# The silu's add of one on POOL in two of four channel blocks, and DMA transposes and DMA adds kept strictly apart

## Chip, cores and metric

The kernel runs on one core of one Trainium2 chip. The metric is the device time of one execution in microseconds (us).

## What is computed

Two sequences of 16000 steps with 512 channels go through a depthwise convolution of three taps, a silu, four stages of residual quantisation with eight code words each, and a second depthwise convolution on the chosen words. Inputs and outputs are bf16.

```python
B, T, D, K = 2, 16000, 512, 3
Nq, C = 4, 8

def reference(x, dw_enc, codebooks, dw_dec):
    ...
    for i in range(K):
        z = z + xp[:, i:i+T, :] * dw_enc[i][None, None, :]
    z = _silu(z)
    res = z
    q = jnp.zeros_like(z)
    for s in range(Nq):
        cb = codebooks[s]
        d2 = jnp.einsum("btd,btd->bt", res, res)[..., None] - 2.0 * jnp.einsum("btd,cd->btc", res, cb) + jnp.einsum("cd,cd->c", cb, cb)[None, None, :]
        idx = d2.argmin(-1)
        sel = cb[idx]
        q = q + sel
        res = res - sel
    qp = jnp.pad(q, ((0,0),(pad,pad),(0,0)))
    for i in range(K):
        y = y + qp[:, i:i+T, :] * dw_dec[i][None, None, :]
    return y
```

## The kernel before

**Tiles.** The 32000 steps are 250 groups of 128, cut into 16 chunks: one of 12 groups, fourteen of 16, one of 14 (which is treated as 16 in the first part). Channels lie on the partitions in four blocks (`i` from 0 to 3), so a tile of one block of one chunk is 128 x 2048.

**The first part, `front`.** For each chunk, DMA transposes on the SP queue bring the input from HBM with channels on partitions into XT (`run`, L486, up to four groups each, two XT buffers; 74 in all and one edge). Chunk 0 is transposed by PE instead. Then, for each of the four blocks (`block`): DVE multiplies by the three taps (`product`, L553, out to Z and to two tiles T); the products are added up (`total`), by DVE (L561) or by an accumulating DMA on the POOL queue (L559). From chunk 1 on (`EARLY = 1`) the first of a block's two sums is a DMA in all four blocks and the second in block 3 (`DMA_ADDS`): five a chunk, 75 in all. The silu follows as exp on ACT (L565, E from Z), an add of one on DVE (`one`, L569, E in place), a logarithm on ACT (L573, LN from E), exp of its negative on ACT (L576), and the product with Z on DVE (`silu`, L581, into RES).

**The second part, `stage`, four times a chunk.** PE scores the residual against the code words (L643, into PS), DVE takes norm and products out (L651, L654), combines them (L673, L679, L684), finds the least (L689) and writes a one-hot row (L697), which PE turns (L707) and DVE copies (L714). PE then multiplies it with the words; the residual RES is brought up to date either by DVE (L747, from SEL in PSUM) or by PE and an ACT copy (L752, L758). At the end `outputs` decodes on PE (L785), copies with ACT to YSB (L791, three buffers) and stores from the SP queue (L795).

**The order of the work.** It is planned ahead, when the program is built. Every step is a task with an engine, the time that it holds the engine, the time until its result is there, and a due time (`Plan.add`). `pass_over` plays the tasks through forwards or backwards by rank; `run` repeats that for each entry of `ROUNDS` (a seed, two spreads for the random shift of the ranks, and a number of passes), each from the order of the one before. `emit` writes the instructions out in the order of planned starts, and each engine runs its own in that order. All DMAs are one engine of the plan, "DMA". Transposes are of kind 1 there (`RUNS`), accumulating DMAs of kind 2 (`ADDS`), stores of none; between a DMA of one kind and one of the other the plan leaves `APART` us, and weighs such a pause with `CLUMP` when it picks. A picked DMA is listed at the moment when it is picked, the pause included in the time that it holds the plan's engine. POOL is an engine of the plan of its own, though the accumulating DMAs are issued from its queue.

`keep_apart` makes the program hold to that on the chip: a transpose waits for an accumulating DMA, and the other way round, where `others` are those of the other kind issued so far.

```python
if len(others) >= LAG:
    tc.add_manual_dep(t.ins, others[-LAG].name, ...)
mine.append(t.ins)
```

With `LAG = 2` it waits for the last but one of the other kind.

Of the kernel before, what the change touches and what calls it, by code (L numbers as in the profile page):

```python
# [13 lines left out]
ALU = mybir.AluOpType  # L14
# [21 lines left out]

EARLY = 1

RUN = 4

AHEAD = 40
# [2 lines left out]
PERIOD, LEAD, STAGE, LATE, SPREAD = 56, 0.4, 0.9, 0.3, 0.3  # L44
FAR = -3.3e38

ROUNDS = [(940, 0.3, 0.0, 7), (4101, 0.3, 2.0, 9), (5991, 0.3, 0.0, 7), (15520, 0.3, 0.0, 10)]


CELLS, COLUMNS, ROWS = range(3)  # L50
WHOLE = (CELLS, CELLS, 0, 0.0)
SWITCH, CLING, SLOW = 0.1, 10.0, 1.08
RUNS, ADDS = (1, 1, 0, 0.0), (2, 2, 0, 0.0)
APART, CLUMP = 0.5, 2.0

LAG = 2


class Plan:
# [18 lines left out]
    def pass_over(self, rank, backward=False):  # L78

        tasks = self.tasks  # L80
        needs = [t[3] for t in tasks]
        after = [[] for _ in tasks]
        for n, ds in enumerate(needs):
            for d in ds:
                after[d].append(n)
        if backward:
            needs, after = after, needs
        takes, gives = (7, 6) if backward else (6, 7)
        left = [len(d) for d in needs]
        engines = list(dict.fromkeys(t[0] for t in tasks))  # L90
        ready = {e: [] for e in engines}
        until = {e: 0.0 for e in engines}
        slots = dict(self.slots)
        for n, t in enumerate(tasks):
            if not left[n]:
                heapq.heappush(ready[t[0]], (rank[n], n))
        now, events, order, starts, before = 0.0, [], [], [0.0] * len(tasks), WHOLE
        sort, ended = 0, 0.0
        while True:
            going = True  # L100
            while going:
                going = False
                for e in engines:
                    if until[e] > now + 1e-9:
                        continue
                    passed, pick, least, gap = [], None, 0.0, 0.0
                    while e == "DMA" and ready[e]:
                        at, n = heapq.heappop(ready[e])
                        passed.append((at, n))
                        if all(slots[k] > 0 for k in tasks[n][takes]):  # L110
                            kind, lost = tasks[n][8][0], 0.0
                            if kind and sort and kind != sort:
                                lost = max(0.0, APART - (now - ended))
                            if pick is None or at + CLUMP * lost < least:
                                pick, least, gap = n, at + CLUMP * lost, lost
                    while e == "PE" and ready[e]:
                        at, n = heapq.heappop(ready[e])
                        passed.append((at, n))
                        if all(slots[k] > 0 for k in tasks[n][takes]):
                            here = tasks[n][8]  # L120
                            lost = self.between(here, before) if backward else self.between(before, here)
                            if pick is None or at + CLING * lost < least:
                                pick, least, gap = n, at + CLING * lost, lost
                    if pick is not None:
                        passed = [v for v in passed if v[1] != pick]
                        if e == "PE":
                            before = tasks[pick][8]
                        elif tasks[pick][8][0]:
                            sort, ended = tasks[pick][8][0], now + gap + tasks[pick][1]
                    while pick is None and ready[e]:  # L130
                        at, n = heapq.heappop(ready[e])
                        if all(slots[k] > 0 for k in tasks[n][takes]):
                            pick = n
                            break
                        passed.append((at, n))
                    for p in passed:
                        heapq.heappush(ready[e], p)
                    if pick is None:
                        continue
                    t = tasks[pick]  # L140
                    for k in t[takes]:
                        slots[k] -= 1
                    order.append(pick)
                    starts[pick] = now
                    until[e] = now + gap + t[1]
                    heapq.heappush(events, (now + gap + t[1], -1))
                    heapq.heappush(events, (now + gap + max(t[1], t[2]), pick))
                    going = True
            if len(order) == len(tasks):
                return starts, order  # L150
            now = events[0][0]
            while events and events[0][0] <= now + 1e-9:
                _, n = heapq.heappop(events)
                if n < 0:
                    continue
                for k in tasks[n][gives]:
                    slots[k] += 1
                for a in after[n]:
                    left[a] -= 1
                    if not left[a]:  # L160
                        heapq.heappush(ready[tasks[a][0]], (rank[a], a))
# [46 lines left out]
def kernel(  # L208
# [8 lines left out]
    nc = tc.nc  # L217
# [255 lines left out]
    def load(st, org):  # L473
        plan.part += 1
        g0, G, GP = st["g0"], st["G"], st["GP"]
        done = []
        if g0 == 0:
            load_rows(st, org)
            return

        def place():
            st["XT"] = xpool.tile([P, GC + 2, KT, P], BF16, name="XT")

        def run(n, m):
            g = g0 + n - 1
            t = nc.sync.dma_start_transpose(out=st["XT"][:, n:n + m, :, :].rearrange("p n i t -> p (n i) t"),  # L486
                                        in_=xv[:, g:g + m, :].rearrange("p g d -> p (g d)"))
            keep_apart(t, runs, adds)

        def edge(n):  # L490
            st["XE"] = const.tile([P, KT, P], BF16, name="XE")
            keep_apart(nc.sync.dma_start_transpose(out=st["XE"], in_=group_rows(0)), runs, adds)

        def shift(n):
            XT, XE = st["XT"], st["XE"]
            nc.gpsimd.tensor_copy(XT[:, n, :, 0:P - 1], XE[:, :, 1:P])
            for b in range(B):
                p = (b + 1) * HB - 1
                nc.gpsimd.memset(XT[:, n, :, p:p + 1], 0.0)
            if GP > G:  # L500
                nc.gpsimd.memset(XT[:, G + 2:GP + 2, :, :], 0.0)

        def behind():
            nc.gpsimd.tensor_copy(st["XT"][0:1, 0, 0, 0:2], XR[0:1, 1, 0:2])
            nc.gpsimd.tensor_copy(st["XT"][0:1, 0, 0, 2:4], CB4[0:1, 0:2])
            for b in range(B):
                p = b * HB + 32
                nc.gpsimd.tensor_copy(st["XT"][p:p + 1, 0, 0, 0:2], XR[p:p + 1, 0, 0:2])

        room = plan.add("SP", 0.0, 0.0, [], org - 2.2 * PERIOD, place, take=("XT",))  # L510
        if st["n"] == 1:
            room = plan.add("POOL", 0.8, 1.0, [room, book, chunks[0]["rows"]], early, behind)
            gate.append(room)
        inside = min(G + 2, S + 1 - g0)
        for n in range(0, G + 2, RUN):
            due = org - 2.2 * PERIOD + 0.01 * n
            m = min(RUN, inside - n)
            if m > 0:
                done.append(plan.add("DMA", 0.7 * m, 2.7 + 0.7 * m, [room], due, lambda n=n, m=m: run(n, m), mode=RUNS))
        if inside < G + 2:  # L520
            t = plan.add("DMA", 0.9, 3.2, [room], due, lambda: edge(G + 1), mode=RUNS)
            st["edge"] = plan.add("POOL", 1.0, 1.4, [t], due, lambda: shift(G + 1))
        st["loaded"] = done + [st.get("edge")]

    def front(st, org):
        n, G, MB = st["n"], st["GP"], st["MB"]
        f = G / GC

        def dve(full):
            return 0.1 + (full - 0.1) * f  # L530
# [14 lines left out]
        def block(i):  # L545
            plan.part += 1
            u = {}

            def product(k):
                name = "ZTU"[k]  # L550
# [15 lines left out]

            def one():
                e = u["E"][:, 0:G, :]
                nc.vector.tensor_scalar(out=e, in0=e, scalar1=1.0, scalar2=None, op0=ALU.add)  # L569

            def log():
                u["LN"] = lnpool.tile([P, GC, P], F32, name="LN")
# [25 lines left out]
            st["taps"].append(t)  # L598
            z = add_up(2, [z, t])
            e = plan.add("ACT", act(1.8), act(1.8) + 0.12, [z], due, exp, take=("E",))  # L600
            e = plan.add("DVE", dve(0.6), dve(0.6) + 0.1, [e], due, one)
            e = plan.add("ACT", act(1.8), act(1.8) + 0.12, [e], due, log, take=("LN",))
            e = plan.add("ACT", act(1.8), act(1.8) + 0.12, [e], due, inverse, give=("LN",))
            r = plan.add("DVE", dve(1.13), dve(1.13) + 0.1, [e] + [t for t in st["silu"][-1:]], due, silu,
# [285 lines left out]
```

## Time and profile before

| | |
|---|---|
| median of three runs | 744.69 us (741.8 to 744.74) |
| the profiled execution's own time | 742.04 us |
| span of that execution | 740.3 us |
| granted PE clock, mean | 0.934 |
| adds of one on DVE (L569) | 64, of which 60 of 128x2048 |
| accumulating DMAs (L559) | 75, 512 KB each |
| transposes (L486) | 74 |

Lines of the profile that begin with L and a number are groups of instructions: line of the kernel, engine, operation, what is written and read, their shapes and count, then busy time in us and the mean of one in ns, then the engine's idle time just ahead of them and what ended it. Times in the timeline are start and length in us. POOLq and SPq are the issuing queues of these engines.

### The profile page before, as it was taken

What the parts mean: (1) busy time and instruction counts of PE and PEld (TensorE: products, weight loads), DVE (VectorE), ACT (ScalarE), POOL (GpSimd) and SP (SyncE); (2) the same over time, 40 slices, a digit from 0 to 9 for tenths busy, and PEclk for the clock granted to TensorE, in tenths of its full rate; (3) what the DMA queues carried; (4) which work ended last, traced back from release to release, by engine and by line L of the source; (5) the groups of instructions that cost most, each with busy time, mean ns of one, the idle gap of its engine ahead of it and who ended that gap; (6) DMA issues with size and microseconds to landing.
All of it is one profiled execution on the core that took longest, in us unless ns stands there. A gap on an engine that the chain in (4) does not pass through costs nothing. (4 is left out here: it accounts for less than half of the span.)

```text
span 740.3 us, 23586 instructions
## 1 busy us (share of the span) xinstructions
PE 590.8 (80%) x10478; PEld 314.2 (42%) x10544; DVE 685.9 (93%) x1359; ACT 665.4 (90%) x539; POOL 81.7 (11%) x104
## 2 busy tenths in 40 slices
PE   5037687787987888986978888878988898989996
PEld 5023334344444444434444444444453444444543
DVE  6999989899999999997999999989999999998952
ACT  2688979899999999998899999989999999976576
POOL 3112101111101011100101111100111101100000
PEclk9566969999999999999799899999999999999999
DMA  7969795859696967839978875959896435320234
GB/s 178 189 130 182 135 200 104 141 122 201 182 174 158 209 133 164 165 116 143 188 171 177 175 165 143 182 132 174 172 210 136 131 64 152 87 88 2 88 143 199
DMA packets 160833, 111.14 MB, mean 150 GB/s; under 512 B 142426, under 2 KB 142811, under 8 KB 160603
## 3 DMA queue, kind: packets, MB, share of 16 engines
q1 hardware_dynamic: 148976, 69.61, 39.5%
q0 software_dynamic: 11472, 39.76, 29.9%
q8 instruction: 82, 1.34, 0.8%
q10 hardware_dynamic: 282, 0.26, 0.1%
q14 instruction: 21, 0.16, 0.1%
HBM read 2.39 MB, written 32.77 MB: 47 GB/s over the span
## 5 line engine op out<-in xcount | busy, mean ns | idle before, releaser
L758 ACT ACTIVATE RES<-NEW 128x1024 bf16<-128x1024 f32 (+1 forms) x218 | 218.5, 1043 | 28.6 <-PE NEW L731 21.9
L747 DVE TENSOR_TENSOR RES<-RES,SEL 128x1024 bf16<-128x1024 bf16 (+1 forms) x166 | 197.5, 1203 | 6.7 <-PE SEL L731 6.3
L643 PE MATMUL PS<-RES 128*64 128x80 bf16 (+1 forms) x8064 | 176.1, 203 | 11.2 <-DVE RES L581 9.7
L643 PEld LDWEIGHTS <-RES 128*64 128x64 bf16 x8064 | 172.8, 115 | 19.6 <-DVE RES L581 10.6
L752 PE MATMUL NEW<-RES,IDENT 128*128 128x512 bf16 (+1 forms) x436 | 137.7, 399 | 31.3 <-ACT RES L758 15.6
L791 ACT ACTIVATE YSB<-Y 128x1024 bf16<-128x1024 f32 (+1 forms) x126 | 126.6, 1061 | 8.4 <-PE Y L785 4.5
L565 ACT ACTIVATE E<-Z 128x2048 bf16<-128x2048 bf16 (+1 forms) x64 | 123.2, 1931 | 11.5 <-DMA Z<-T 4.0
L559 POOL DMA_DIRECT2D Z<-T x75 | 72.9, 976 | 537.5 <-ACT RES L758 78.8
L573 ACT ACTIVATE LN<-E 128x2048 f32<-128x2048 bf16 (+1 forms) x64 | 123.0, 1923 | 9.9 <-DVE E L569 9.2
L576 ACT ACTIVATE E<-LN 128x2048 bf16<-128x2048 f32 (+1 forms) x64 | 123.0, 1922 | 0.4
L651 DVE TENSOR_REDUCE TR<-PS 128x5 bf16<-128x320 f32 (+1 forms) x188 | 96.0, 515 | 14.4 <-PE PS L643 14.3
L553 DVE TENSOR_SCALAR T<-XT,WENC 128x2048 bf16<-128x2048 bf16 (+1 forms) x128 | 94.8, 745 | 5.1 <-DMA Z<-T 5.1
L731 PEld LDWEIGHTS <-CBN 32*128 32x128 bf16 x768 | 32.6, 92 | 137.7 <-issue 134.3
L785 PE MATMUL Y<-A,OHT 128*128 128x512 bf16 x219 | 77.6, 382 | 16.4 <-ACT RES L758 6.0
L731 PE MATMUL NEW<-OHT,CBN 32*128 32x512 bf16 (+1 forms) x436 | 88.3, 402 | 0.1
L581 DVE TENSOR_TENSOR RES<-Z,E 128x2048 bf16<-128x2048 bf16 (+1 forms) x64 | 77.3, 1208 | 0.0
L731 PE MATMUL SEL<-OHT,CBN 32*128 32x512 bf16 (+1 forms) x332 | 58.7, 396 | 22.0 <-ACT RES L758 13.3
L637 PE MATMUL PS<-MASK,IDENT 128*64 128x320 bf16 (+1 forms) x376 | 64.6, 340 | 8.6 <-DVE PR L654 6.2
L561 DVE TENSOR_TENSOR Z<-Z,T 128x2048 bf16<-128x2048 bf16 (+1 forms) x53 | 62.5, 1181 | 2.7 <-DMA Z<-T 2.7
L752 PEld LDWEIGHTS <-IDENT 128*128 128x128 bf16 x436 | 33.1, 99 | 67.4 <-issue 57.4
L430 PE MATMUL PS<-MASK,IDENT 128*128 128x384 bf16 x167 | 46.2, 359 | 10.1 <-DVE PR L654 9.8
L785 PEld LDWEIGHTS <-OHT 128*128 128x128 bf16 x373 | 32.1, 97 | 50.8 <-issue 22.8
(78 smaller groups left out, 416.2 us busy)
## 6 DMA issues: line engine op xcount, KB each, us to landing
Z<-T POOLq DMA_DIRECT2D x75, 512.0 KB, 5.6
out_dram<-YSB SPq DMA_DIRECT2D x61, 512.0 KB, 3.2
RES<-in_x_dram SPq DMA_DIRECT2D x1, 1664.0 KB, 6.8
XT<-in_x_dram SPq DMA_TRANSPOSE x74, 5.7
out_dram<-YSB SPq DMA_DIRECT2D x1, 384.0 KB, 2.3
out_dram<-YSB SPq DMA_DIRECT2D x1, 256.0 KB, 2.7
A<-in_dw_dec_dram POOLq DMA_DIRECT2D x2, 96.0 KB, 6.4
CB<-in_codebooks_dram ACTq DMA_DIRECT2D x1, 128.0 KB
```

The costliest lines, as they stand in the source:

```text
L553: nc.vector.tensor_scalar(out=places(u[name]), in0=taps(i, k), scalar1=WENC[:, i, k:k + 1], scalar2=None, op0=ALU.mult)
L565: nc.scalar.activation(u["E"][:, 0:G, :], u["Z"][:, 0:G, :], ACT.Exp, scale=-1.0)
L573: nc.scalar.activation(u["LN"][:, 0:G, :], u["E"][:, 0:G, :], ACT.Ln)
L576: nc.scalar.activation(u["E"][:, 0:G, :], u["LN"][:, 0:G, :], ACT.Exp, scale=-1.0)
L643: nc.tensor.matmul(V[h * HT:(h + 1) * HT, r, :], lhsT=half[:, LC:LC + HT], rhs=half[:, lo:hi], start=False, stop=(i == KT - 1), skip_group ...
L651: nc.vector.tensor_reduce(out=u["TR"][:, q:q + m], in_=u["V", q][:, :, own:own + HT], axis=AX.X, op=ALU.max)
L731: nc.tensor.matmul(ps, lhsT=CBN[s][rows, i * P:(i + 1) * P], rhs=u["OHT"][rows, 0:MB, :], start=start, stop=True, skip_group_check=True)
L747: nc.vector.tensor_tensor(out=old, in0=old, in1=u["SEL", i, j][:, :, 0:W].rearrange("p h (m t) -> p h m t", t=HT), op=ALU.add)
L752: nc.tensor.matmul(NEW[:, h, 0:W], lhsT=IDENT, rhs=tokens(i, j + h, 1), start=True, stop=False, skip_group_check=True)
L758: nc.scalar.activation(old, u["NEW", i, j][:, :, 0:W].rearrange("p h (m t) -> p h m t", t=HT), ACT.Copy)
L785: nc.tensor.matmul(Y[:, h, :], lhsT=lhs(), rhs=rhs, start=(a == 0), stop=(a == len(terms) - 1))
L791: nc.scalar.activation(u["YSB"][:, k:k + n, :], u[k][:, 0:n, :], ACT.Copy)
```

## The change

Four things are changed together.

- In blocks 0 and 2, from chunk 1 on, the silu's add of one is issued on POOL instead of DVE: 30 instructions. The plan gives it 2.4 us there and 0.3 more until the result is used.
- `LAG` goes from 2 to 1: each transpose waits for the latest accumulating DMA, and each accumulating DMA for the latest transpose, so that the two kinds are never under way together.
- The plan's pause between kinds goes from 0.5 us to 1.9 us for a transpose behind an accumulating DMA and 2.3 us the other way round, and its costs of a transpose of m groups from 0.7 m (and 2.7 us until landing) to 0.6 m (and 2.4).
- `ROUNDS` has seven other entries in place of four, so the order of all instructions is another.

```diff
+ONE_ON_POOL = (0, 2)
+POOL_ONE = 2.4
...
-ROUNDS = [(940, 0.3, 0.0, 7), (4101, 0.3, 2.0, 9), (5991, 0.3, 0.0, 7), (15520, 0.3, 0.0, 10)]
+ROUNDS = [(845, 0.3, 0.0, 3), (1649, 0.3, 2.0, 7), (1998, 3.0, 0.0, 4), (2046, 0.3, 0.0, 9), (2092, 0.3, 2.0, 8), (2574, 1.0, 3.0, 6), (4809, 0.3, 0.0, 6)]
...
-APART, CLUMP = 0.5, 2.0
-
-LAG = 2
+APART = (0.0, 1.9, 2.3)
+CLUMP = 2.0
+
+LAG = 1
...
                             if kind and sort and kind != sort:
-                                lost = max(0.0, APART - (now - ended))
+                                lost = max(0.0, APART[sort if backward else kind] - (now - ended))
...
-                done.append(plan.add("DMA", 0.7 * m, 2.7 + 0.7 * m, [room], due, lambda n=n, m=m: run(n, m), mode=RUNS))
+                done.append(plan.add("DMA", 0.6 * m, 2.4 + 0.6 * m, [room], due, lambda n=n, m=m: run(n, m), mode=RUNS))
...
+            on_pool = st["n"] >= EARLY and i in ONE_ON_POOL
...
-                nc.vector.tensor_scalar(out=e, in0=e, scalar1=1.0, scalar2=None, op0=ALU.add)
+                where = nc.gpsimd if on_pool else nc.vector
+                where.tensor_scalar(out=e, in0=e, scalar1=1.0, scalar2=None, op0=ALU.add)
...
-            e = plan.add("DVE", dve(0.6), dve(0.6) + 0.1, [e], due, one)
+            if on_pool:
+                e = plan.add("POOL", dve(POOL_ONE), dve(POOL_ONE) + 0.3, [e], due, one)
+            else:
+                e = plan.add("DVE", dve(0.6), dve(0.6) + 0.1, [e], due, one)
```

## The prediction

> **What bounds the kernel now.** I read the page's busy line first, then a table of busy time in three stretches, then the groups by shape, the waits, the DMA queues, and last the timeline round the few places where POOL computes.
>
> ```profile
> span 740.3 us, 23586 instructions
> PE 590.8 (80%) x10478; PEld 314.2 (42%) x10544; DVE 685.9 (93%) x1359; ACT 665.4 (90%) x539; POOL 81.7 (11%) x104
> core 0: us, PE busy (x) PEld busy (x) DVE busy (x) ACT busy (x) POOL busy (x), PEclk, DMA share, GB/s
> 0.00:140.00 140.00, 84.98 (x1270) 46.70 (x1271) 126.80 (x250) 107.34 (x76) 25.19 (x42) 0.77 0.85 158
> 140.00:640.00 500.00, 420.16 (x7696) 222.55 (x7747) 487.20 (x956) 486.18 (x394) 55.83 (x62) 0.97 0.75 158
> 640.00:741.00 101.00, 85.66 (x1518) 44.97 (x1528) 71.88 (x155) 71.86 (x71) 0.69 (x1) 0.99 0.27 101
> ```
>
> In the 500 us in the middle DVE works 487.2 and ACT 486.2: 12.8 and 13.8 us are idle. Both engines are full, and a plan that takes time from one of them alone has some 13 us to win there. In the first 140 us DVE (126.8) is the fuller of the two, and in the last 101 us neither is (71.9 each). PE (420 of 500) and POOL (56 of 500) are not bounds. So the question is what the change does to DVE's time, and whether ACT, equally full, lets any gain through.
>
> **The add of one: what DVE gives up.** The add of one (L569) of blocks 0 and 2 goes to POOL in chunks 1 to 15: 30 instructions of 128x2048.
>
> ```profile
> L569 DVE TENSOR_SCALAR E<-E 128x2048 bf16<-128x2048 bf16 x60 | 41.6, 693 | 0.5 <-ACT E L565 0.5
> 564.24 0.60 DVE E L569
> 564.85 0.22 DVE KEY L684
> ```
>
> One is recorded with 693 ns, but records on DVE overlap by some 0.09 us: in the chain of waits it holds the engine for 0.60 us before the next starts. DVE gives up 30 x 0.60 = **18.0 us**.
>
> **What POOL takes for it.** No POOL arithmetic of this size is in the trace. The nearest rows are copies:
>
> ```profile
> L496 POOL COPY XT<-XE 128x508 bf16<-128x508 bf16 x1 | 0.6, 610 | 13.4 <-DMA XE<-in_x_dram 13.4
> L505 POOL COPY XT<-CB 1x2 bf16<-1x2 bf16 x1 | 0.2, 175 | 0.8 <-DMA CB<-in_codebooks_dram 0.8
> ```
>
> (610 - 175) / 506 is 0.86 ns an element, so 2048 elements take 175 + 2046 x 0.86 = 1.93 us, and 2.46 us if the 610 ns are simply scaled. I take 1.93, as two copies give a fixed part; the planner's constant says 2.4. 30 of them are 58 us on an engine that is idle for 659 of 740: POOL's own time costs nothing. What follows it does: the logarithm (L573) of that block waits 1.3 us longer than for DVE's 0.60, unless ACT has other work queued ahead, which the plan arranges.
>
> **What DVE pays for it.** DVE and POOL get in each other's way, in both directions:
>
> ```profile
> 556.75 0.61 POOL L496 COPY XT<-XE 128x508 bf16<-128x508 bf16 x1 [13.38 <-DMA XE<-in_x_dram]
> 555.88 1.21 DVE L747 TENSOR_TENSOR RES<-RES,SEL 128x1024 bf16<-128x1024 bf16 x1
> 557.01 1.43 DVE L581 TENSOR_TENSOR RES<-Z,E 128x2048 bf16<-128x2048 bf16 x1
> 31.69 2.00 POOL L559 DMA_DIRECT2D Z<-T  x1 [16.44 <-DVE E L569]
> 32.40 0.74 DVE L553 TENSOR_SCALAR T<-XT,WENC 128x2048 bf16<-128x2048 bf16 x1
> 33.06 0.55 DVE L569 TENSOR_SCALAR E<-E 128x1536 bf16<-128x1536 bf16 x1
> L559 POOL DMA_DIRECT2D Z<-T x75: 860/862/2004, 31.7 to 639.5; - x75
> ```
>
> First: the one POOL copy of size ran to 557.36. The silu product (L581, both inputs in SBUF) was free to start at 557.09, when L747 ended, and took 1.43 instead of the 1.23 that its group has below: 0.20 us more, nearly the 0.27 us for which POOL was still at it. L747, with one input in PSUM, ran beside the same copy in its usual 1.21. Second, the other way round: issuing an accumulating DMA holds POOL for 0.86 us, but 2.00 us in the issue within which L553 and L569 ran, and those two kept their times. So products, adds of one and two-input operations on SBUF exclude POOL's work, and whoever came second waited.
>
> How often DVE comes second follows from the groups. Those that exclude POOL:
>
> ```profile
> L553 DVE TENSOR_SCALAR T<-XT,WENC 128x2048 bf16<-128x2048 bf16 x120 | 90.0, 753 | 5.1 <-DMA Z<-T 5.1
> L553 DVE TENSOR_SCALAR Z<-XT,WENC 128x2048 bf16<-128x2048 bf16 x60 | 45.1, 752 | 0.0
> L581 DVE TENSOR_TENSOR RES<-Z,E 128x2048 bf16<-128x2048 bf16 x60 | 73.5, 1226 | 0.0
> L561 DVE TENSOR_TENSOR Z<-Z,T 128x2048 bf16<-128x2048 bf16 x45 | 55.0, 1222 | 2.7 <-DMA Z<-T 2.7
> L679 DVE TENSOR_TENSOR KEY<-V,GPOS 128x128 bf16<-128x128 bf16 x60 | 18.2, 304 | 0.2
> L684 DVE SCALAR_TENSOR_TENSOR KEY<-KEY,RANK 128x128 bf16<-128x128 bf16 x60 | 18.2, 303 | 0.2
> L673 DVE TENSOR_TENSOR V<-PR,TR 128x128 bf16<-128x128 bf16 x60 | 17.5, 291 | 0.2
> L697 DVE TENSOR_TENSOR OH<-KEY,M 128x128 bf16<-128x128 f32 x60 | 17.4, 290 | 0.1
> ```
>
> With L569 these are 585 instructions. Those that should not (an input in PSUM, or one plain input):
>
> ```profile
> L747 DVE TENSOR_TENSOR RES<-RES,SEL 128x1024 bf16<-128x1024 bf16 x156 | 188.4, 1219 | 6.4 <-PE SEL L731 6.3
> L651 DVE TENSOR_REDUCE TR<-PS 128x5 bf16<-128x320 f32 x120 | 58.6, 492 | 8.2 <-PE PS L643 8.1
> L651 DVE TENSOR_REDUCE TR<-PS 128x6 bf16<-128x384 f32 x68 | 37.8, 556 | 6.3 <-PE PS L643 6.2
> L714 DVE COPY OHT<-ps_oh 128x512 bf16<-128x512 bf16 x60 | 25.4, 424 | 3.0 <-PE ps_oh L707 3.0
> L654 DVE CAST PR<-PS 128x40 bf16<-128x40 f32 x120 | 23.7, 198 | 0.0
> L654 DVE CAST PR<-PS 128x48 bf16<-128x48 f32 x68 | 14.0, 206 | 0.0
> L689 DVE TENSOR_REDUCE M<-KEY 128x16 f32<-128x128 f32 x60 | 17.1, 284 | 0.1
> ```
>
> These are 652 with 365 us, 0.56 each and 0.47 without the overlap of records. So 1.11 of them, 0.52 us, stand between one excluding instruction and the next. An add of one on POOL starts when the current excluding instruction ends, DVE goes on for about 0.55 us, and then stands until POOL is done: 1.93 - 0.55 = 1.4 us. Where two L747 follow one another (2.3 us) it loses nothing; for that I take a tenth off: 1.25 us, 30 times, **37.5 us**. Against the 18.0 given up, DVE has 19.5 us more to do, in stretches where it has 2.6% idle. The ends: no loss at all (POOL gives way each time, as in issuing), net -18.0; and with 2.46 us on POOL, 30 x 1.85 - 18 = +37.5.
>
> A rule weighed here: the Trainium skill, page "SBUF — State Buffer", section "Who interferes with whom", says that the port pair shared by VectorE and GpSimd is locked for a whole instruction by whichever issues first, and that the other blocks fully. The 0.20 of 0.27 us agrees; as a price, the row alone bears out only a third of the copy's length (0.20 of 0.61), which over 1.93 us would be 0.63 us and 19 us in all, a net of +1, where the rule gives the +19.5.
>
> **Transposes and adds kept apart (LAG 2 to 1).** Each transpose on SP now waits for the latest accumulating DMA to land, each accumulating DMA on POOL for the latest transpose; before, for the one before it.
>
> ```profile
> DMA to landing us min/median/max: 4.5/5.6/12.3
> 333.23 15.48 SPq L486 DMA_TRANSPOSE XT<-in_x_dram  x3
> 333.51 0.86 POOL L559 DMA_DIRECT2D Z<-T  x1 [4.18 <-DVE OH L697]
> 345.82 0.75 DVE L553 TENSOR_SCALAR T<-XT,WENC 128x2048 bf16<-128x2048 bf16 x1 [4.21 <-DMA Z<-T]
> SPq L486 <- DMA Z<-T: 100.7, 18, 13.7
> DVE T L553 <- DMA Z<-T: 5.1, 4, 4.2
> ```
>
> The first line is for the adds (L559). The add issued at 333.51, beside the transpose at 333.23, is the one that kept DVE for 4.21 us until 345.82, 12.3 us after its issue; alone an add takes 4.5. The new waits take that case away. DVE's idle time on adds, 5.1 + 2.7 (L561, above) = **7.8 us**, can go; to the other side, each change of kind now costs a landing, some 2 us planned, and DMA has cover for it: its share is 0.75 in the middle with the overlaps stretched. Behind a waiting transpose on SP stand the stores, with three YSB buffers; behind a waiting accumulating DMA on POOL stand, newly, the adds of one. I take the whole 7.8 as gained and price the wait on POOL as a rival. Bounds: -7.8 to +15 (below). The order itself is planned anew (seven rounds); it moves work within 13 us of slack in the middle and I give it nothing.
>
> **Sum.** The profiled execution took 742.04 us (span 740.3), 2.65 under the median 744.69 of three. -18.0 + 37.5 - 7.8 = +11.7: 753.7 in its terms, **756** for a median.
>
> **The rivals.** *POOL gives way.* If the add of one waits for DVE as the issues did, DVE loses 18.0, and ACT is the bound. ACT's idle 13.8 us in the middle are the most that can go: 742 - 13 + 2.65 = 732. For it: 2.00 against 0.86 us, with L553 at 0.74 and L569 unharmed. Against it: L581 at 1.43. Any stall under about 0.6 us an add, half of my value (30 x 0.6 - 18.0 - 7.8 = -7.8), ends here too, at 732 to 740. Chance 0.34.
>
> *The parts cancel.* With a stall of 0.8 us, 24.0 - 18.0 - 7.8 = -1.8, or 743. Chance 0.08.
>
> *An add of one stands behind a waiting DMA on POOL.* The plan lists an accumulating DMA before the pause that it gives it, so an add of one that is due within that pause queues behind it, and ACT, in order, stands at L573. If half of the 30 wait 2 us beyond plan, 30 us, of which ACT's slack hides half, it is +15 on my forecast: 771. For it: POOL's idle time ahead of L559 is 7 us a DMA (537.5 over 75).
>
> ```profile
> L559 POOL DMA_DIRECT2D Z<-T x75 | 72.9, 976 | 537.5 <-ACT RES L758 78.8 <-DVE M L689 69.1 <-DVE PR L654 60.8
> ```
>
> Against it: the plan knows these pauses. It decides once L573 waits for POOL over 14 us in all. Chance 0.12.
>
> **How the numbers follow.** My forecast, DVE stalled by POOL, has 0.46, with a range of its own of 749 to 765. With the POOL queue's case, slower by over 0.5% (3.7 us, about what a measurement can tell here) has 0.58, within it 0.08, faster 0.34. Both signs hold much, so the range reaches from 731 (all of ACT's slack used) to 774 (POOL at 2.46 us with the gain on DMA: 742 + 37.5 - 7.8 + 2.65); above lies the POOL queue's case at its worst.
>
> **What would show it.** Right: 30 POOL operations on E of 1.9 us or more; L553, L581 and L561 with means up, their longest records near 2.5 us and more, while L747 and L651 keep theirs; DVE busy above 686; no Z<-T landing over 6 us or so, and no DVE wait on it. Wrong: POOL operations on E stretched to 3 us with L553 and L581 unchanged, and DVE near 668 (the first rival); or L573 waiting for POOL for tens of us with DVE's means unchanged (the third).

## The result and the profile after

| | before | after |
|---|---|---|
| median | 743.25 us (739.93 to 744.74) | 845.74 us (843.05 to 847.57) |
| ratio | | 1.138 (95% interval 1.133 to 1.144) |
| profiled span | 740.3 us | 845.8 us |

The change costs 102 us. The forecast had the direction and the place, not the size: 756, with 774 as its upper end. (Of the runs further below, one execution each of *after_lag2*, *yb2* and *side_copy* counts as slow and is left out of their times.)

The page's span and busy line of the kernel after, and the middle one of its three stretches (busy us of PE, weight loads, DVE, ACT, POOL, then granted PE clock, DMA share, GB/s):

```profile
span 845.8 us, 23638 instructions
PE 639.0 (76%) x10545; PEld 333.5 (39%) x10545; DVE 770.0 (91%) x1329; ACT 670.2 (79%) x539; POOL 245.2 (29%) x134
140.00:640.00 500.00, 396.75 (x6499) 201.76 (x6499) 473.08 (x791) 417.95 (x334) 158.31 (x71) 0.86 0.66 143
```

DVE is busy for 770.0 us where it was 685.9, with fewer instructions, while ACT has the work it had (670.2 after 665.4) and now stands idle for 82 of the 500 us in the middle. The granted PE clock is lower too, 0.86 in the middle where it was 0.97, as it is in every slower run here (0.91 in *lag1_only*); PE is idle for 103 of those 500 us, and no run tests what the clock adds. The groups by shape say which DVE instructions grew (the lines have moved: L553 is L558, L569 is L575, L581 is L587, L561 is L566, L697 is L706, L747 is L756):

```profile
L575 POOL TENSOR_SCALAR E<-E 128x2048 bf16<-128x2048 bf16 x30 | 166.7, 5556 | 177.9 <-ACT E L570 177.9
L575 DVE TENSOR_SCALAR E<-E 128x2048 bf16<-128x2048 bf16 x30 | 20.6, 685 | 2.0 <-ACT E L570 2.0
L558 DVE TENSOR_SCALAR T<-XT,WENC 128x2048 bf16<-128x2048 bf16 x120 | 140.2, 1172 | 2.3 <-DMA Z<-T 2.3
L558 DVE TENSOR_SCALAR Z<-XT,WENC 128x2048 bf16<-128x2048 bf16 x60 | 55.4, 924 | 0.0
L587 DVE TENSOR_TENSOR RES<-Z,E 128x2048 bf16<-128x2048 bf16 x60 | 83.1, 1385 | 0.6 <-issue 0.4 <-ACT E L582 0.2
L566 DVE TENSOR_TENSOR Z<-Z,T 128x2048 bf16<-128x2048 bf16 x45 | 61.7, 1371 | 9.7 <-DMA Z<-T 9.6
L706 DVE TENSOR_TENSOR OH<-KEY,M 128x128 bf16<-128x128 f32 x60 | 24.4, 406 | 0.2
L756 DVE TENSOR_TENSOR RES<-RES,SEL 128x1024 bf16<-128x1024 bf16 x156 | 187.8, 1216 | 9.3 <-PE SEL L740 8.9
```

An add of one takes POOL 5.56 us in the mean (5.35 at the least), not 1.93. The products into T went from 753 to 1172 ns in the mean (50 us over 120), those into Z from 752 to 924, the two-input operations on SBUF from 1226, 1222 and 290 to 1385, 1371 and 406. L756, with an input in PSUM, kept its 1.22. DVE was relieved of 30 adds, 18.0 us by the prediction (their records shrink by 21.0, but records overlap), and is still busy for 84.1 more, so it stands for some 102 us, **3.4 us an add of one**. DVE's idle time grows by 21 us besides (75.8 after 54.4). Three of the thirty in the timeline (start, length, engine and line):

```profile
65.21 5.36 POOL L575 TENSOR_SCALAR E<-E 128x2048 bf16<-128x2048 bf16 x1 [3.51 <-ACT E L570]
65.86 5.25 DVE L558 TENSOR_SCALAR T<-XT,WENC 128x2048 bf16<-128x2048 bf16 x1
211.35 5.35 POOL L575 TENSOR_SCALAR E<-E 128x2048 bf16<-128x2048 bf16 x1 [13.56 <-ACT E L570]
211.87 4.19 DVE L587 TENSOR_TENSOR RES<-Z,E 128x2048 bf16<-128x2048 bf16 x1
642.12 5.35 POOL L575 TENSOR_SCALAR E<-E 128x2048 bf16<-128x2048 bf16 x1 [7.70 <-ACT E L570]
641.83 2.34 DVE L756 TENSOR_TENSOR RES<-RES,SEL 128x1024 bf16<-128x1024 bf16 x2
644.87 1.22 DVE L756 TENSOR_TENSOR RES<-RES,SEL 128x1024 bf16<-128x1024 bf16 x1 [0.18 <-PE SEL L740]
```

In the first, a product came 0.65 us into POOL's add, waited until POOL was done at 70.57 and ended at 71.11: 5.25 us for work of 0.75. In the second a two-input operation waited too, but not to the end. In the third DVE happened to have three L756 and lost nothing.

The trace of all thirty shows the same. 27 adds kept DVE waiting and three did not. Against the medians of the kernel before, 32 DVE instructions took 103 us more: 15 products and two copies within SBUF (L821), which waited for POOL's end, and 15 two-input operations. Of these, 13 began 1.87 us before POOL's end, if they took their usual time once begun; the other two stood behind a copy that waited.

The waits on DMA changed as well. Waits by engine, who ended them, total us, count, longest; the first line is that of the kernel before, the last tells of the adds' landing:

```profile
POOL Z L559 <- DMA XT<-in_x_dram: 7.9, 1, 7.9
POOL Z L564 <- DMA XT<-in_x_dram: 53.7, 7, 12.2
SPq L490 <- DMA Z<-T: 379.8, 33, 25.0
DVE Z L566 <- DMA Z<-T: 9.6, 6, 3.2
DVE T L558 <- DMA Z<-T: 2.3, 3, 1.4
DMA to landing us min/median/max: 4.5/4.9/8.8
```

Adds land sooner once they are issued (median 4.9 after 5.6 us, longest 8.8 after 12.3), but are issued later, behind transposes (53.7 us of waiting at the head of POOL's queue, where 7.9 stood before), and DVE waits for them a little longer than before (11.9 us after 7.8).

### The profile page after: what moved, and what is told of

Its sections match the earlier page's. It is cut to its first block, busy times and chain, and to the rows that moved or that the text cites. A ratio compares the mean times of both kernels' runs of the same rounds, so it can differ in the third digit from the quotient of the medians.

```text
span 845.8 us, 23638 instructions
## 1 busy us (share of the span) xinstructions
PE 639.0 (76%) x10545; PEld 333.5 (39%) x10545; DVE 770.0 (91%) x1329; ACT 670.2 (79%) x539; POOL 245.2 (29%) x134
## 4 chain that ended last, share of the span: by engine, by line
DVE 50%; PE 20%; issue 11%; DMA 10%; ACT 7%; POOL 1%; SPq 0%; ACTq 0%; DVEq 0%; POOLq 0%
DVE RES L756 10%; DVE T L558 10%; DMA Z<-T 7%; PE PS L652 6%; DVE RES L587 6%; DVE Z L566 6%; DVE TR L660 4%; DVE Z L558 4%; PE NEW L761 4%; PE Y L794 3%; ACT RES L767 2%; PE NEW L740 2%; PE PS L646 2%; DMA XT<-in_x_dram 2%; ACT YSB L800 2%
## 5 line engine op out<-in xcount | busy, mean ns | idle before, releaser
L575 POOL TENSOR_SCALAR E<-E 128x2048 bf16<-128x2048 bf16 x30 | 166.7, 5556 | 177.9 <-ACT E L570 177.9
L756 DVE TENSOR_TENSOR RES<-RES,SEL 128x1024 bf16<-128x1024 bf16 (+1 forms) x166 | 197.1, 1200 | 9.3 <-PE SEL L740 8.9
L652 PE MATMUL PS<-RES 128*64 128x80 bf16 (+1 forms) x8064 | 193.3, 211 | 13.5 <-DVE RES L587 9.6
L652 PEld LDWEIGHTS <-RES 128*64 128x64 bf16 x8064 | 189.7, 122 | 23.9 <-DVE RES L587 10.4
L761 PE MATMUL NEW<-RES,IDENT 128*128 128x512 bf16 (+1 forms) x436 | 149.0, 428 | 41.8 <-ACT RES L767 18.4
L558 DVE TENSOR_SCALAR T<-XT,WENC 128x2048 bf16<-128x2048 bf16 (+1 forms) x128 | 145.0, 1137 | 2.3 <-DMA Z<-T 2.3
L579 ACT ACTIVATE LN<-E 128x2048 f32<-128x2048 bf16 (+1 forms) x64 | 120.9, 1888 | 25.0 <-POOL E L575 19.6
L660 DVE TENSOR_REDUCE TR<-PS 128x5 bf16<-128x320 f32 (+1 forms) x188 | 95.3, 511 | 23.7 <-PE PS L652 23.4
L794 PE MATMUL Y<-A,OHT 128*128 128x512 bf16 x249 | 87.4, 401 | 14.3 <-ACT RES L767 5.6
L587 DVE TENSOR_TENSOR RES<-Z,E 128x2048 bf16<-128x2048 bf16 (+1 forms) x64 | 87.0, 1359 | 0.6 <-issue 0.4
L740 PE MATMUL SEL<-OHT,CBN 32*128 32x512 bf16 (+1 forms) x332 | 64.2, 433 | 27.1 <-DVE RES L756 14.3
L566 DVE TENSOR_TENSOR Z<-Z,T 128x2048 bf16<-128x2048 bf16 (+1 forms) x53 | 69.2, 1308 | 9.7 <-DMA Z<-T 9.6
L558 DVE TENSOR_SCALAR Z<-XT,WENC 128x2048 bf16<-128x2048 bf16 (+1 forms) x64 | 57.9, 904 | 0.0
```

The costliest lines, as they stand in the source:

```text
L558: nc.vector.tensor_scalar(out=places(u[name]), in0=taps(i, k), scalar1=WENC[:, i, k:k + 1], scalar2=None, op0=ALU.mult)
L575: where.tensor_scalar(out=e, in0=e, scalar1=1.0, scalar2=None, op0=ALU.add)
L579: nc.scalar.activation(u["LN"][:, 0:G, :], u["E"][:, 0:G, :], ACT.Ln)
L587: nc.vector.tensor_tensor(out=st["RES"][:, i, 0:2 * G, LC:LC + HT], in0=halves(u["Z"]), in1=halves(u["E"]), op=ALU.mult)
L652: nc.tensor.matmul(V[h * HT:(h + 1) * HT, r, :], lhsT=half[:, LC:LC + HT], rhs=half[:, lo:hi], start=False, stop=(i == KT - 1), skip_group ...
L660: nc.vector.tensor_reduce(out=u["TR"][:, q:q + m], in_=u["V", q][:, :, own:own + HT], axis=AX.X, op=ALU.max)
```

## Experiments

The kernel before took 743.6 to 744.5 us beside them. A ratio has its 95% interval behind it.

**The parts one by one.** *pool_only*: only the engine of the 30 adds changes, in the order of before.

```diff
-                nc.vector.tensor_scalar(out=e, in0=e, scalar1=1.0, scalar2=None, op0=ALU.add)
+                where = nc.gpsimd if st["n"] >= EARLY and i in (0, 2) else nc.vector
+                where.tensor_scalar(out=e, in0=e, scalar1=1.0, scalar2=None, op0=ALU.add)
```

> The kernel before with one edit: the 30 adds of one are issued on POOL, in the order that was planned with them on DVE. Theory 1 (DVE stands still while POOL works): each add is about 5.4 us on POOL and costs DVE about 3.4 us in L553, L581, L561 and the small two-input operations, 103 us in all, less 18 given up: 743 + 85 = 828, to 845 as ACT now also waits for POOL where the plan did not know of it. DVE busy 765 to 775. Theory 2 (the strict separation and the new order cost most of it): under 800.

Measured: 843.61 us, ratio 1.135 (1.131 to 1.139), at the top of theory 1's range. This single edit costs as much as the whole change. The last line is that of the kernel after.

```profile
PE 641.0 (76%) x10544; PEld 336.2 (40%) x10544; DVE 779.4 (93%) x1329; ACT 670.2 (80%) x539; POOL 245.5 (29%) x134
ACT LN L574 <- POOL E L570: 39.2, 12, 6.9
ACT LN L579 <- POOL E L575: 19.6, 11, 3.9
```

DVE is busy for 779.4 us, a little above the 765 to 775 expected; ACT also waits 39 us for POOL's results in an order that was not planned for them (19.6 in the kernel after), yet the time is the same.

*after_dve*: the kernel after, the adds of one back on DVE.

```diff
-                where = nc.gpsimd if on_pool else nc.vector
+                where = nc.vector
```

> The kernel after with one edit: the 30 adds of one are issued on DVE, at the places in the order that were planned for POOL; waits and order else as after. Theory 1: the loss goes nearly whole, 738 to 755, DVE busy about 688, no L558 over 0.8 us. Theory 2: 790 or more.

Measured: 777.04 us, 1.046 (1.038 to 1.053): between the two theories. 69 us of the 102 go; DVE's busy time is back at 689.7. 33 us stay that POOL's adds do not explain.

```profile
PE 614.2 (79%) x10545; PEld 323.0 (42%) x10545; DVE 689.7 (89%) x1359; ACT 667.3 (86%) x539; POOL 76.8 (10%) x104
DVE Z L566 <- DMA Z<-T: 16.2, 10, 3.7
DVE T L558 <- DMA Z<-T: 6.4, 3, 4.3
```

*lag1_only*: the kernel before with `LAG = 1`.

> The kernel before with one edit: each transpose and each accumulating DMA waits for the latest of the other kind (LAG 1), in the order planned with pauses of 0.5 us. Theory 1: 738 to 752: adds land in under 5 us in the median and DVE's 7.8 us of idle time on them changes by a few us either way. Theory 2: 760 or more, with DVE and ACT idle for tens of us on Z<-T.

Measured: 787.05 us, 1.058 (1.054 to 1.063), theory 2's number. DVE's work is unchanged (687.5 us), its waits are not:

```profile
POOL Z L559 <- DMA XT<-in_x_dram: 55.1, 5, 15.9
DVE Z L561 <- DMA Z<-T: 33.8, 16, 5.5
DVE T L553 <- DMA Z<-T: 11.7, 4, 5.6
ACT E L565 <- DMA Z<-T: 13.4, 5, 6.9
SPq L486 <- DMA Z<-T: 270.3, 28, 20.0
389.63 13.52 SPq L486 DMA_TRANSPOSE XT<-in_x_dram  x2
394.79 1.75 POOL L559 DMA_DIRECT2D Z<-T  x2 [9.20 <-ACT E L565]
399.40 1.23 DVE L561 TENSOR_TENSOR Z<-Z,T 128x2048 bf16<-128x2048 bf16 x1 [4.00 <-DMA Z<-T]
```

DVE waits 45.5 us for adds where it waited 7.8. The last three lines show one case: a transpose goes out at 389.63 (the row's 13.52 us take in the next one too), an add only at 394.79, once the transpose has landed, and DVE then stands for 4.00 us until the add is there. The row names an exp of ACT that ended 0.09 us before; but the trace has the transpose's landing at 394.24, and 15 of the adds start like this, 0.56 us behind one. 28 transposes in turn waited for the landing of an add, where 18 did before. A change of kind now costs a whole flight (the time from issue to landing), 4.6 us here, before the next DMA may start.

*after_lag2*: the kernel after with `LAG = 2`.

> The kernel after with one edit: LAG 2 again. Theory 1: 840 to 852, as the waits are not what costs. Theory 2: falls by 30 us or more.

Measured: 846.98 us, 1.136 (1.128 to 1.143), as theory 1 has it: with POOL's adds in place the strict waits cost nothing that can be seen. So the parts do not add up (100 and 43 alone, 102 with the new order together). With the same order and waits, DVE's waits for adds are 22.6 us in *after_dve* and 11.9 in the kernel after: where DVE stands for POOL anyway, an add that comes late has more often landed by the time that DVE asks for it. This fits, but no run tests it by itself.

**Waits or order?** *after_dve_lag2*: the last two edits together, in the order of after.

> The kernel after in its order, but the adds of one issued on DVE and LAG 2. With LAG 1 this kernel took 777. Theory W (the stricter waits cost the 33 us): 743 to 755. Theory O (the order planned for POOL's adds costs them): 770 to 780.

Measured: 760.92 us, 1.024 (1.017 to 1.030). Of after_dve's 33 us, 16 go when the waits are loosened and 17 stay, which leaves the order; the time lies between the ranges of theories W and O. DVE's waits for adds hardly differ between the two profiled executions (22.6 and 20.5 us); its waits for PE's scores at L660 do (29.5 and 19.9). So how the strict waits reach the time in this order stays open. *replan_dve* and *replan_dve_lag2* plan the adds of one on DVE, so that the order fits:

```diff
-ONE_ON_POOL = (0, 2)
+ONE_ON_POOL = ()
```

> The kernel after with all adds of one on DVE in the plan as well, so that the order fits: LAG 1, pauses of 1.9 and 2.3 us and the seven rounds as after. Theory W (strict separation costs even where it is planned for): 760 to 785, DVE idle on Z<-T for 15 us or more. Theory O (only the misfit of order cost): 735 to 750.

> As the run before (all adds of one on DVE, planned so with the longer pauses), but LAG 2. Theory W: 735 to 755, clearly below the run with LAG 1. Theory O: the same as with LAG 1, within 6 us.

Measured: 789.63 us (1.060, 1.053 to 1.066) with LAG 1, 766.78 us (1.029, 1.022 to 1.036) with LAG 2. Theory O falls: a fitting order doesn't help, and strict separation costs 23 us though its pauses were planned for. Both runs missed their ranges from above, so theory W has the sign and not the size: the new pauses and rounds give an order that is 23 us worse than before's even with before's waits.

*lag3_only* and *lag5_only* loosen the waits in the kernel before.

> The kernel before with one edit: LAG 3, so that a transpose or an accumulating DMA waits for the last but two of the other kind. Theory W (the wait for the latest one delays adds behind whole runs of transposes; it, and not the overlap, is what costs): LAG 1 took 43 us more than LAG 2, and LAG 3 takes no more than LAG 2, 730 to 746, with fewer waits on Z<-T. Theory S (overlap costs as well, 2 is the best of both): 750 or more, with landings of Z<-T over 6 us in the median.

> The same with LAG 5, so that the two kinds are hardly held apart. Theory W: 728 to 746. Theory S: slower than LAG 3, 755 or more.

Measured: 742.79 us, 1.001 (0.998 to 1.004), and 746.62 us, 1.005 (1.001 to 1.008). With LAG 3 SP waits for adds for 22.8 us instead of 100.7, adds land in 5.8 us in the median, and the time is the same. LAG 5 is slower by half a per cent, just above theory W's range. Theory S falls: overlap costs next to nothing here, waiting for the latest costs much.

**POOL and DVE.** Is it DVE's standing, or that ACT and POOL's queue wait for the result? To make room for a tile of its own, *yb2* plans with two YSB buffers; *side_add* adds to it 30 adds of one on POOL that nobody waits for, *side_copy* 30 copies.

```diff
+                if st["n"] >= EARLY and i in (0, 2):
+                    nc.gpsimd.tensor_scalar(out=SCR, in0=SCR, scalar1=1.0, scalar2=None, op0=ALU.add)
```

> The kernel before with two YSB buffers instead of three, planned for them: it makes room in SBUF for the tile of the two runs that follow and is what they are compared with. 743 to 775.

> As the kernel with two YSB buffers, all adds of one on DVE, plus 30 adds of one on POOL over a tile of 128x2048 of zeros that nothing else reads or waits for, issued behind the exps of blocks 0 and 2. Theory 1 (DVE is kept from its ports while POOL works): 5.4 us each on POOL, 3.0 to 3.8 us each more on DVE, so 85 to 110 us over the kernel with two YSB buffers although no result is waited for. Theory 3 (ACT's wait for POOL's result, and POOL's queue, are what costs): within 15 us of it.

> The same with 30 copies of the tile onto itself on POOL in place of the adds. If a copy of 2048 elements takes 1.9 to 2.0 us, as the copy of 508 would have it, the prediction's own law, length less 0.55 and a tenth off, gives 1.25 us a copy and 38 us over the kernel with two YSB buffers. If the time is set by the count of POOL operations and not by their length: the same as the adds. If copies take 5 us as well, the length was mis-scaled for copies too: 85 to 110.

Measured: 786.51, 897.11 and 819.75 us. yb2 lies above its range and serves only as a base. Busy line and a DVE group of yb2; busy line, POOL's group and the same DVE group of side_add; then for side_copy a row of busy times (PE, weight loads, DVE, ACT, POOL), POOL's group and its lengths in ns (least, median, longest):

```profile
PE 634.0 (80%) x10601; PEld 326.5 (41%) x10601; DVE 691.0 (87%) x1359; ACT 668.4 (85%) x539; POOL 79.8 (10%) x104
L561 DVE TENSOR_TENSOR Z<-Z,T 128x2048 bf16<-128x2048 bf16 x45 | 55.2, 1227 | 0.4 <-DMA Z<-T 0.4
```

```profile
PE 661.5 (74%) x10601; PEld 338.7 (38%) x10601; DVE 810.3 (91%) x1359; ACT 672.2 (75%) x539; POOL 245.7 (27%) x135
L569 POOL TENSOR_SCALAR SCR<-SCR 128x2048 bf16<-128x2048 bf16 x30 | 173.2, 5772 | 0.2
L563 DVE TENSOR_TENSOR Z<-Z,T 128x2048 bf16<-128x2048 bf16 x45 | 75.2, 1671 | 2.2 <-DMA Z<-T 2.2
```

```profile
0.00:900.00 900.00, 636.11 (x10601) 328.25 (x10601) 734.06 (x1359) 668.81 (x539) 139.94 (x135) 0.90 0.59 124
L569 POOL COPY SCR<-SCR 128x2048 bf16<-128x2048 bf16 x30 | 69.7, 2323 | 0.2
L569 POOL COPY SCR<-SCR x30: 1895/2217/3271, 39.8 to 688.4; 128x2048 bf16<-128x2048 bf16 x30
```

Adds that nobody waits for cost 111 us (897.11 - 786.51): theory 3 falls. DVE is busy for 119 us more, 4.0 an add of 5.77 us, a little over the 3.0 to 3.8 of theory 1. A copy of the same size takes 1.90 us at the least, as scaled in the prediction (1.93), 2.32 in the mean; it costs DVE 43 us, 1.44 each, and the time 33 us, 1.1 each (the executions of yb2 lie up to 6 us from their median). So the loss grows with the length of the POOL operation, and near the length that the prediction took its price of 1.25 was about right.

*forms* asks why the add is so much longer than the copy, with six small forms such as

```diff
+        if k == 0:
+            g.tensor_scalar(out=SCRB[:, 0:480], in0=SCRB[:, 0:480], scalar1=1.0, scalar2=None, op0=ALU.add)
+        ...
+        elif k == 3:
+            g.tensor_scalar(out=SCR[:, 0:240], in0=SCR[:, 0:240], scalar1=1.0, scalar2=None, op0=ALU.add)
+        ...
```

> The kernel before plus 30 small POOL operations in six forms, five times each, on a tile that nothing else reads: an add of one to 480 bf16 elements, the same on 240, a copy of 480, an add of one to 240 fp32 elements, a sum of two tensors of 480, and a product with one of 480. Only their lengths are asked for. Theory a (the add itself costs 2.6 ns an element on POOL, whatever the type): add 480 about 1.35 us, 240 bf16 and 240 fp32 about 0.75, copy 0.6. Theory b (bf16 in and out is what is slow): 240 fp32 near 0.4. Theory c (a large fixed part or the waiting for DVE makes the 5.4): add 480 close to the copy.

It was run once (750.31 us); only the lengths are asked for. Lengths in ns (least, median, longest), the last line that of the kernel after:

```profile
L409 POOL TENSOR_SCALAR SCR<-SCR x5: 832/1480/2123, 51.1 to 548.5; 128x240 bf16<-128x240 bf16 x5
L413 POOL TENSOR_SCALAR SCR<-SCR x5: 801/1147/1149, 68.8 to 600.5; 128x240 f32<-128x240 f32 x5
L407 POOL TENSOR_SCALAR SCR<-SCR x5: 1580/1747/2087, 32.7 to 530.6; 128x480 bf16<-128x480 bf16 x5
L411 POOL COPY SCR<-SCR x5: 906/1179/1641, 67.5 to 578.8; 128x480 bf16<-128x480 bf16 x5
L575 POOL TENSOR_SCALAR E<-E x30: 5354/5375/7113, 47.0 to 739.4; 128x2048 bf16<-128x2048 bf16 x30
```

Small POOL operations are often stretched by waiting for DVE, so only the shortest tell. 240 elements take as long in fp32 (0.80) as in bf16 (0.83), against theory b. From 240 to 2048 elements the add grows by (5354 - 832) / 1808 = 2.5 ns an element; the copy grows by (1895 - 610) / 1540 = 0.83 from 508 to 2048. Theory a holds: it is the operation. At 480 elements a product with a constant took 1.74 us at the least, the add 1.58, and a sum of two tensors only 1.31. Why the add is so slow stays open. That the copy of 480 took 0.91 at the least, more than the 0.61 of the 508 in the kernel before, is left open; waiting is the likely reason.

**What the relief alone is worth.** *no_add* frees DVE of the same 30 adds without POOL. The logarithm on ACT adds the one instead, so the sum is rounded differently and the output is not that of the kernel before.

```diff
+                if st["n"] >= EARLY and i in (0, 2):
+                    return
                 nc.vector.tensor_scalar(out=e, in0=e, scalar1=1.0, scalar2=None, op0=ALU.add)
...
-                nc.scalar.activation(u["LN"][:, 0:G, :], u["E"][:, 0:G, :], ACT.Ln)
+                nc.scalar.activation(u["LN"][:, 0:G, :], u["E"][:, 0:G, :], ACT.Ln, bias=1.0 if st["n"] >= EARLY and i in (0, 2) else 0.0)
```

> The kernel before, in its order, with the 30 adds of one of blocks 0 and 2 left out on every vector engine: the logarithm on ACT takes the one as its bias instead, so that DVE is freed of 18 us and POOL is not used. The sum is then rounded differently than in the kernel before. Theory A (DVE bounds the middle, ACT just behind): 728 to 737. Theory B (ACT bounds as much as DVE): 738 to 744, no gain that can be measured.

Measured: 736.99 us, 0.992 (0.986 to 0.998).

```profile
PE 588.4 (80%) x10478; PEld 312.1 (42%) x10544; DVE 671.3 (91%) x1329; ACT 665.3 (90%) x539; POOL 79.4 (11%) x104
140.00:640.00 500.00, 422.92 (x7765) 223.88 (x7820) 478.13 (x934) 488.49 (x395) 55.26 (x62) 0.97 0.76 158
```

Theory A, at its upper end: DVE has 22 us to spare in the middle, ACT only 11.5. In the order of before some 7 us were to be had (1.4 to 10.5 by the interval); an order planned for it was not tried.

## Why the prediction was wrong, point by point

- **What bounds the kernel**: right. DVE and ACT are both full in the middle, and no_add shows that 14.6 us less work on DVE (671.3 after 685.9) give 7.
- **What POOL takes** (1.93 us, with 2.46 as the other end): the term that was mis-sized, and the step that failed. It is 5.36 us. The row it came from was a copy, and copies do scale as worked out (1.90); the add does not run at a copy's pace. Both ends were taken from the same copy, so the range held no other operation's pace. The planner's 2.4 was no better. The upper end has a slip as well: 2.46 less 0.55, with a tenth off, is 1.72 us an add and not 1.85, which gives 770 and not 774. The Trainium skill, page "GPSIMD Engine Reference", section "Engine selection", calls one-input elementwise work on GpSimd roughly line-rate; the copy with its 0.83 ns an element can agree, the add with its 2.5 cannot, and the measurement decides.
- **What DVE pays**: the mechanism was right, and shown in both directions: instructions of the named kinds stood (and a copy, L821, that was not named), L756 did not of itself, and side_add loses the time with no result waited for. The tenth taken off is right too: 3 of 30 adds cost nothing. Put 5.36 in place of 1.93 in the prediction's own working: (5.36 - 0.55) x 0.9 x 30 = 130, less 18.0 and 7.8, is 104 on 742.04, 849 for a median; 846 was measured. That it comes so close is partly luck. DVE stood for 102 us and not 130, 3.4 an add and not 4.3, as two-input operations did not wait for POOL's end; against that, the 7.8 were not gained and DVE is idle for 21 us more.
- **The strict separation** (a gain of 7.8 us): wrong in sign. The reason given, that landings get shorter, came true in part (8.8 us at the longest after 12.3, not the 6 or so named as a sign). The landing that each change of kind costs was named, and put at nothing because DMA's share of 0.75 left cover; but in lag1_only an add stood behind a transpose while DVE waited for it, whatever the share. Alone the separation costs 43 us in before's order, 16 and 23 in orders planned with the longer pauses. In the kernel after this is hidden: LAG 2 gives 847 as well, most likely because DVE stands for POOL meanwhile.
- **The new order** (nothing): with the adds on DVE and LAG 2 it is 17 to 23 us slower than before's. Whether the longer pauses or the other rounds do that was not told apart.
- **Rivals.** POOL gives way: no, DVE stood for 27 of the 30 adds. Adds of one behind a waiting DMA on POOL: ACT's waits for POOL are 19.6 us in the kernel after, over the 14 from which this was to decide, but 39.2 us in pool_only came with the same time, and side_add lost as much with no such wait: the threshold was no test of the cause. In the trace of the kernel after only two of the 30 adds stood behind a DMA, for 2.4 and 1.3 us past the end of their exp; the other 28 started within 0.2 us of it, on an idle POOL. The range's upper end failed with the one length.

## What to carry to other kernels

Before work goes to POOL, time that very operation at that size; one of its copies says nothing of its adds. Price it by what it keeps from DVE, not by POOL's idle time: even at a copy's length, 30 of them cost this kernel 33 us and the adds had held DVE for 18. And a wait that keeps two kinds of DMA apart costs a flight at every change of kind; shorter flights are little gain where the engines had hardly waited for them.

## What the runs showed of the hardware

- On POOL an add with a constant took 2.5 ns for each element of a partition's row, a copy 0.83, in bf16; fp32 made no difference at 240 elements.
- While POOL works on SBUF, a DVE product waited until POOL's end (at 65.86, for an add that ended at 70.57). The two-input L587 at 211.87 ended at 216.06; less its usual 1.22 it began about 214.84, 3.5 us into POOL's 5.35. The Trainium skill, page "SBUF — State Buffer", section "Who interferes with whom", has the pair of ports locked for a whole instruction; here that holds for the products, and the two-input operation was let in earlier.
- Two-input DVE operations that stood for an add on POOL began 1.87 us before its end, as counted above: 13 in the kernel after, 13 in pool_only, 22 in side_add. For a copy on POOL they waited nearly to the end: the 19 in side_copy began 0.13 us before it.
